# Reordering VectorE's queue around transferred states, and a third group of seven-product up tiles, in a one-core SSM + GLU kernel

## The chip, the cores and the metric

One core of one Trainium2 chip. The metric is the device time in microseconds (us) of one execution. All runs told here were in the fast state, with a granted TensorE clock between 0.998 and 1.0. Besides the time, each run gives the **span**: the time from the first to the last instruction that the profile sees.

## The reference, cut to what matters

```python
xn  = layernorm(x)                      # x: 2048 tokens x 512
Bu  = einsum("bld,pd->blp", xn, B_bar)  # complex, 512 states
h   = Lam_bar * h + Bu[:, t]            # 2048 steps in a row
y   = 2 * einsum("blp,dp->bld", hseq, Cmat).real + xn * Dskip
mlp = (silu(xn @ w1) * (xn @ w3)) @ w2  # 512 -> 1792 -> 512
out = x + y + mlp
```

The first part is a state space model (SSM: 512 complex states, stepped through the tokens), the second a gated linear unit (GLU: a gate tile times an up tile, then w2). The kernel takes the tokens in four blocks of 512, each of four chunks of 128. Per block it makes the gate and up tiles (14 of each, 128 features by 512 tokens), rotates the inputs of the states, scans them, rotates them back ("posts": two multiplications and an add per half of the states), and then makes the outputs for two pairs of chunks (pairs 0 to 7 in all) from gated features and states. Several of the products use a seven-product scheme in place of eight: fewer matmuls, more sums on VectorE. An "eviction" is the sum or copy that takes a finished result out of TensorE's accumulation bank.

## The kernel before: what the change and the argument touch

The order of VectorE's instructions is decided while the program is built. Work that can wait stands in a list with an estimated cost; at marked places `fill` takes from the list as long as VectorE, by these estimates, is no more than `lead` ahead of TensorE. VectorE then runs what it got in that order.

```python
class Filler:                       # cut: __init__, first, pop, flush
    def add(self, cost, fn, key=None):
        self.tasks.append((cost, fn, key))
    def tensor(self, us):            # TensorE's own clock, in estimates
        self.pe += us
    def own(self, us, after=0.1):    # an instruction put in directly
        self.dve = max(self.dve, self.pe + after) + us
    def fill(self, lead=None):
        limit = self.pe + (self.lead if lead is None else lead)
        while self.tasks and self.dve + 0.5 * self.tasks[0][0] <= limit:
            ...
            self.pop()
        self.dve = max(self.dve, self.pe - 1.0)
```

The add that ends a post is a transfer with accumulation, issued by GpSimd (`act<-p` in the profile), except for the last half of block 3:

```python
def post_c(csl=slice(0, CPB)):
    a, p16 = act_state(b, hf)[:, csl], st["p16"][:, csl]
    if (b, hf) == (NBLK - 1, 1):
        nc.vector.tensor_tensor(out=a, in0=a, in1=p16, op=ALU.add)
    else:
        gp.dma_start(out=a, in_=p16, accum_op=ALU.add)
```

The sums of a pair of chunks read those states. Two of the three are on VectorE (in pairs 1, 6 and 7 the third as well; that branch is cut):

```python
three = (0.9, subtract(s3, a11, a21), ("sums", n))
two   = (0.9, subtract(s2, s3, a22), ("sums", n))
one   = (0.0, lambda: gp.dma_start(out=a21, in_=a22, accum_op=ALU.add), ("sums", n))
```

The last block's gate and up stage: plain tiles first, then `NG` groups of four up tiles by seven products each. `s4` and the two adds (evictions that `add` makes) are on VectorE between the products that need them:

```python
for n in range(NG):
    ...
    product(g, a11, b11, True);  copy(f, g)
    product(e, s1n, t1, True);   copy(s5, e)
    gate_side(f0, upper[0])
    bg.fill(1.2)
    gates.pop()()
    product(f, a12, b21, False)
    product(g, s2n, t2, False);  copy(e, g)
    bg.own(0.42)
    nc.vector.tensor_tensor(out=s4n, in0=a12, in1=s2n, op=ALU.subtract)
    ...
    gate_side(f0 + 1, upper[0])
    bg.fill()
    product(g, s3n, t3, False);  copy(z, g)
    add(lower[1][:, :, TH:TBLK], g)
    product(e, s4n, b22, False)
    add(upper[1][:, :, TH:TBLK], e)
    ...
```

Where pair 4's sums are put in the list (`middle` comes between the rotations of block 3's first half and those of its second, two multiplications each; `between` comes after both):

```python
last_posts = ssm_tasks(3, middle=[(0.0, after_y2, None), *row_sums(4, *pairs[4])])
```

## Time and profile before

| | before |
|---|---|
| time, median of the first 3 runs | 202.15 us (202.10 to 202.42) |
| span of the profiled run | 200.7 us |
| TensorE busy | 195.3 us, 97% |
| VectorE busy | 179.6 us, 89%, 256 instructions |
| ScalarE busy | 134.5 us, 67% |
| first gate matmul of block 0 | starts at 12.80 us |
| last matmul | starts at 197.74 us |

What lies before the first gate matmul (loads, layernorm, transposes) came out between 12.2 and 13.1 us in the profiles of this study, whatever the kernel. From that matmul to the start of the last one, which I call the **steady stretch**, the kernel before takes 197.74 - 12.80 = 184.94 us. Three more profiles of the same schedule give 185.03, 184.94 and 185.04. A change of 0.1 us can be read from it, while the times of one kernel's runs in one call lie 0.3 to 1.2 us apart.

The views that carry the prediction are shown in it. One more belongs here, the first line of the chain that ended last, as shares of the span:

```profile
PE 86%; DMA 5%; DVE 5%; issue 1%; SPq 1%; DVEq 0%
```

The 5% of DMA and the 5% of DVE say that the end of the program hangs somewhere on VectorE and on transfers, and not on matmuls alone.

### The profile page before, as it was taken

To read this page: it belongs to the slowest core of one execution; us is meant where nothing else is said; L and a number is where in the kernel's file an instruction comes from. 1 tells how busy PE (TensorE), PEld (TensorE's weight loads), DVE (VectorE), ACT (ScalarE), POOL (GpSimd) and SP (SyncE) were. 2 spreads that over 40 slices of the span, in tenths; PEclk is the share of its full clock that TensorE was granted. 3 is DMA by queue.
4 is the path that set the end of the run, shared out by engine and by line. 5 is a ranking of instruction groups with operands and counts; after the bars stand their busy time and mean duration, and the time that the engine had idled before them with its cause. 6 is when DMAs were issued, how large, how long until landed. Compare 5 with 4: busy or idle time off the path is not lost.

```text
span 200.7 us, 3660 instructions
## 1 busy us (share of the span) xinstructions
PE 195.3 (97%) x1376; PEld 129.4 (64%) x1389; DVE 179.6 (89%) x256; ACT 134.5 (67%) x279; POOL 49.9 (25%) x75
## 2 busy tenths in 40 slices
PE   8899999999999999999999999999999999999994
PEld 2774444444444488855565478888445568888893
DVE  3599699999999999989899998999996989999952
ACT  4699797699999987868997674451668783111220
POOL 7170279800411143031202115030032103310000
PEclk9999999999999999999999999999999999999999
DMA  6999995990398046721997187747159511990111
GB/s 165 321 265 221 303 169 112 339 278 7 57 180 152 0 91 121 131 81 32 171 114 104 30 152 129 172 75 105 52 73 178 111 28 30 187 159 30 52 41 42
DMA packets 32514, 25.38 MB, mean 126 GB/s; under 512 B 16240, under 2 KB 30192, under 8 KB 32496
## 3 DMA queue, kind: packets, MB, share of 16 engines
q0 software_dynamic: 6384, 11.64, 34.2%
q1 hardware_dynamic: 25536, 13.21, 27.4%
q10 hardware_dynamic: 576, 0.30, 0.7%
q8 instruction: 11, 0.18, 0.4%
q14 instruction: 7, 0.06, 0.1%
HBM read 7.74 MB, written 2.10 MB: 49 GB/s over the span
## 4 chain that ended last, share of the span: by engine, by line
PE 86%; DMA 5%; DVE 5%; issue 1%; SPq 1%; DVEq 0%
PE gu_ps L580 33%; PE gu_ps L1039 17%; PE y_ps L1039 10%; PE bu_ps L1039 7%; PE y_ps L450 3%; PE bu_ps L450 3%; PE y_ps L766 3%; DMA act<-p 3%; DMA w_sb<-in_B_w_dram 2%; PE gu_ps L834 2%; PE gu_ps L612 2%; PE gu_ps L766 2%; PE bu_ps L766 1%; PE y_ps L855 1%; PE bu_ps L612 1%
## 5 line engine op out<-in xcount | busy, mean ns | idle before, releaser
L580 PE MATMUL gu_ps<-xnT,w_sb 128*128 128x512 bf16 x304 | 68.9, 379 | 0.4
L580 PEld LDWEIGHTS <-w_sb 128*128 128x128 bf16 x312 | 30.5, 98 | 34.2
L1039 PEld LDWEIGHTS <-act 128*128 128x128 f16 x462 | 43.5, 98 | 5.5
L589 ACT ACTIVATE g<-gu_ps 128x512 bf16<-128x512 f32 x41 | 24.8, 604 | 5.2 <-PE gu_ps L580 3.2
L590 ACT ACTIVATE u<-gu_ps 128x512 bf16<-128x512 f32 x41 | 24.9, 606 | 4.8 <-PE gu_ps L580 4.5
L503 DVE TENSOR_TENSOR_SCAN u<-rho,ends,u 128x512 bf16<-128x512 f32 x16 | 20.2, 1274 | 0.0
L834 PE MATMUL gu_ps<-xnT,w_sb 128*128 128x512 bf16 x77 | 18.4, 379 | 0.2
L525 POOL DMA_DIRECT2D act<-p x7 | 9.2, 1316 | 36.3 <-DVE act L517 25.2
L1039 PE MATMUL gu_ps<-w_sb,act 128*128 128x256 bf16 (+3 forms) x126 | 15.9, 267 | 0.0
L597 DVE TENSOR_TENSOR act<-g,u 128x1024 f16<-128x1024 bf16 x21 | 14.3, 679 | 0.0
L834 PEld LDWEIGHTS <-w_sb 128*128 128x128 bf16 x80 | 7.8, 98 | 7.5
L846 ACT ACTIVATE g<-gu_ps 128x512 bf16<-128x512 f32 x14 | 8.4, 598 | 6.1 <-PE gu_ps L834 6.0
L450 PEld LDWEIGHTS <-bt 128*128 128x128 bf16 x64 | 6.3, 98 | 7.5
L1039 PE MATMUL bu_ps<-w_sb,act 128*128 128x256 bf16 (+3 forms) x84 | 10.4, 264 | 0.0
L1062 ACT ACTIVATE x_blk<-gu_ps 128x256 f32<-128x256 f32 (+1 forms) x9 | 3.3, 366 | 10.6 <-PE gu_ps L1039 10.6
L1039 PE MATMUL gu_ps<-ct,act 128*128 128x256 f16 (+1 forms) x72 | 10.4, 267 | 0.0
L993 POOL DMA_DIRECT2D act<-act x5 | 4.6, 926 | 21.8 <-DVE tw L986 10.3
L503 DVE TENSOR_TENSOR_SCAN u<-rho,u 128x512 bf16<-128x512 f32 x8 | 9.2, 1207 | 0.0
L1039 PEld LDWEIGHTS <-x_blk 128*128 128x128 f16 x88 | 8.6, 98 | 1.0
L1039 PEld LDWEIGHTS <-tw 128*128 128x128 f16 x88 | 8.6, 98 | 1.0
L486 DVE TENSOR_TENSOR u<-u,tabe 128x2048 bf16<-128x2048 bf16 x7 | 8.6, 1223 | 0.2
L511 DVE TENSOR_TENSOR p<-u,tabe 128x2048 f16<-128x2048 bf16 x7 | 8.5, 1221 | 0.1
(203 smaller groups left out, 384.4 us busy)
## 6 DMA issues: line engine op xcount, KB each, us to landing
act<-p POOLq DMA_DIRECT2D x7, 512.0 KB, 5.8
xn<-x_blk POOLq DMA_DIRECT2D x4, 512.0 KB, 5.5
out_dram<-xn SPq DMA_DIRECT2D x15, 128.0 KB, 1.7
w_sb<-in_B_w_dram SPq DMA_DIRECT2D x1, 1792.0 KB, 8.6
act<-act POOLq DMA_DIRECT2D x5, 352.0 KB, 4.3
w_sb<-in_B_w_dram SPq DMA_DIRECT2D x2, 768.0 KB, 6.1
u<-p POOLq DMA_DIRECT2D x3, 512.0 KB, 5.6
w_sb<-in_B_w_dram SPq DMA_DIRECT2D x4, 256.0 KB, 4.7
```

Source lines behind the costliest of these rows:

```text
L450: nc.tensor.matmul(out=ps, lhsT=bt[:, ri, dt, pt * P:(pt + 1) * P], rhs=xnT_blk[b][:, dt, :], start=(dt == 0), stop=(dt == NDT - 1))
L486: nc.vector.tensor_tensor(out=st["g"], in0=st["g"], in1=tabe[:, psl, 0:1, :].to_broadcast(FULL), op=ALU.mult)
L503: nc.vector.tensor_tensor_scan(out=v, data0=rho[:, pt:pt + 1].to_broadcast([P, TBLK]), data1=v, initial=init, op0=ALU.mult, op1=ALU.add)
L511: nc.vector.tensor_tensor(out=by_state(st["p16"][:, csl]), in0=by_chunk(st["g"][:, :, ::-1, tsl]), in1=by_chunk(tabe[:, psl, 2:0:-1, tsl]) ...
L525: gp.dma_start(out=a, in_=p16, accum_op=ALU.add)
L580: nc.tensor.matmul(out=ps[:, tsl], lhsT=w[:, dt, f * P:(f + 1) * P], rhs=xnT[:, dt, tsl], start=(dt == 0), stop=(dt == NDT - 1))
L589: nc.scalar.activation(out=g16[:, f % 2, :], in_=g_ps, func=ACT.Silu)
L590: nc.scalar.activation(out=u16[:, f % 2, :], in_=u_ps, func=ACT.Copy)
L597: nc.vector.tensor_tensor(out=act_gates(b, f - 1), in0=split(g16), in1=split(u16), op=ALU.mult)
L766: nc.tensor.matmul(out=out[:, h * TH:(h + 1) * TH], lhsT=left[:, h, k, :], rhs=right[:, k, :], start=(start and h == 0 and k == 0), stop=( ...
L834: nc.tensor.matmul(out=ps, lhsT=w[:, dt, f * P:(f + 1) * P], rhs=xnT[:, dt, :], start=(dt == 0), stop=(dt == NDT - 1))
L1039: nc.tensor.matmul(out=out, lhsT=left[:, k, :], rhs=right[k][:, cols], start=(start and k == 0), stop=(k == NK - 1), skip_group_check=True)
```

## The change

The intent: take a wait for a transfer out of VectorE's in-order queue by putting pair 4's sums (and in block 2, pair 2's) behind work that needs no transfer; spread block 3's posts so that pair 6 waits for half of them only; and use the seven-product scheme on 12 up tiles instead of 8. Some estimates of the list are lowered, too.

```diff
-    NG = 2
+    NG = 3
-    LEAD = 2.0
+    LEAD = 1.7
 ...  (post_c)
-                if (b, hf) == (NBLK - 1, 1):
+                if b == NBLK - 1 and (hf == 1 or csl.start > 0):
                     nc.vector.tensor_tensor(out=a, in0=a, in1=p16, op=ALU.add)
 ...  (block 3's posts)
-        add(*post0, *scans1)
-        early, late = ([... for fn in post1] for h in range(2))
-        for t in early:
+        def by_tokens(fns, h):
+            part = slice(h * CPB // 2, (h + 1) * CPB // 2)
+            return [(0.0 if fn is post0[2] and h == 0 else 0.6, lambda fn=fn: fn(part), ("ssm", b)) for fn in fns]
+        for t in by_tokens(post0, 0):
             bg.add(*t)
-        return late
+        add(*scans1)
+        for t in by_tokens(post1, 0):
+            bg.add(*t)
+        return by_tokens(post0, 1) + by_tokens(post1, 1)
 ...  (up groups)
-            bg.fill(1.2)
+            bg.fill(0.8)
 ...  (order of the lists)
-    ssm_tasks(2, between=[(0.2, lambda: keep_ends(1)), *row_sums(2, *pairs[2])], late=res_list(3) + column_sums(3))
+    ssm_tasks(2, between=res_list(3), late=[(0.2, lambda: keep_ends(1)), *row_sums(2, *pairs[2]), *column_sums(3)])
-    last_posts = ssm_tasks(3, middle=[(0.0, after_y2, None), *row_sums(4, *pairs[4])])
+    last_posts = ssm_tasks(3, between=[(0.0, after_y2, None), *row_sums(4, *pairs[4])])
```

Cut: the estimated costs of four kinds of work (posts, column sums, pair sums, input sums), lowered by 0.04 to 0.2; a branch that is never taken; and a table `ORDER` whose entries are the order that was already used.

More of the change, by code (lines that the diff above doesn't have):

```diff
@@ L475, in pre_a @@
                     st["p"] = up.tile(FULL, BF16, name="u")
-                elif b > 3:
-                    st["p"] = x_blk[b].rearrange("p (j r) t -> p j r t", r=2)
                 elif b == NBLK - 1:
@@ L538, in add @@
             for fn in fns:
-                bg.add(0.0 if fn in transfers else 1.2, fn,
+                bg.add(0.0 if fn in transfers else 1.2 if fn in scans0 or fn in scans1 else 1.16, fn,
                        ("scan", b) if fn in scans0 else ("post", b) if fn in post0 else ("ssm", b))
@@ L565, in ssm_tasks @@
             return
-        add(*post0, *scans1)
-        early, late = ([(0.6, lambda fn=fn, h=h: fn(slice(h * CPB // 2, (h + 1) * CPB // 2)), ("ssm", b)) for fn in post1]
-                       for h in range(2))
-        for t in early:
+        def by_tokens(fns, h):
+            part = slice(h * CPB // 2, (h + 1) * CPB // 2)
+            return [(0.0 if fn is post0[2] and h == 0 else 0.6, lambda fn=fn: fn(part), ("ssm", b)) for fn in fns]
+        for t in by_tokens(post0, 0):
             bg.add(*t)
-        return late
+        add(*scans1)
+        for t in by_tokens(post1, 0):
+            bg.add(*t)
+        return by_tokens(post0, 1) + by_tokens(post1, 1)
     def glu(b):
@@ L705, in column_sums @@
         run.ready = lambda: ("norm", b, CPB - 1) in sins_done
-        return [(1.7, run, "cols")]
+        return [(1.5, run, "cols")]
     def column_list(b):
@@ L743, in bu_sums @@
         first = [t for two in zip(tasks[0], cols) for t in two]
-        return [(0.42, lambda out=out, x=x, y=y, op=op: nc.vector.tensor_tensor(out=out, in0=x, in1=y, op=op), ("bu", hf))
+        return [(0.36, lambda out=out, x=x, y=y, op=op: nc.vector.tensor_tensor(out=out, in0=x, in1=y, op=op), ("bu", hf))
                 for hf, part in ((0, first), (1, tasks[1])) for out, x, y, op in part]
@@ L986, in subtract @@
             return lambda: nc.vector.tensor_tensor(out=out, in0=x, in1=z, op=ALU.subtract)
-        three = (0.9, subtract(s3, a11, a21), ("sums", n))
-        two = (0.9, subtract(s2, s3, a22), ("sums", n))
+        three = (0.84, subtract(s3, a11, a21), ("sums", n))
+        two = (0.84, subtract(s2, s3, a22), ("sums", n))
         if n in (1, 6, 7):
-            one = (0.9, lambda: nc.vector.tensor_tensor(out=a21, in0=a21, in1=a22, op=ALU.add), ("sums", n))
+            one = (0.84, lambda: nc.vector.tensor_tensor(out=a21, in0=a21, in1=a22, op=ALU.add), ("sums", n))
         else:
@@ L1019 @@
     later = {}
+    ORDER = {4: (1,4,2,6,5,7,3), 5: (1,4,2,6,5,7,3), 6: (1,4,2,6,5,7,3)}
     def y_fast(n, then=(), between=()):
@@ L1131, in y_fast @@
         products = (product1, product2, product3, product4, product5, product6, product7)
-        for i in ((1, 5, 2, 6, 4, 3, 7) if b == 0 else (1, 2, 4, 6, 5, 7, 3) if b == 1 else (1, 4, 2, 6, 5, 7, 3)):
+        for i in ((1, 5, 2, 6, 4, 3, 7) if b == 0 else (1, 2, 4, 6, 5, 7, 3) if b == 1 else ORDER.get(n, (1, 4, 2, 6, 5, 7, 3))):
             if i == 3 and n in LATER:
```

## The prediction

> **What bounds the kernel now.** I read the page first, the engines' busy shares and the 40 slices.
>
> ```profile
> PE 195.3 (97%) x1376; PEld 129.4 (64%) x1389; DVE 179.6 (89%) x256; ACT 134.5 (67%) x279; POOL 49.9 (25%) x75
> PE   8899999999999999999999999999999999999994
> DVE  3599699999999999989899998999996989999952
> ```
>
> TensorE is busy in every slice from the second to the last but one, and VectorE is close behind. Since a busy TensorE may still be waiting inside its modelled ends, I looked next at who waited for whom, for TensorE alone:
>
> ```profile
> PE bu_ps L196 <- PEq L1253: 0.8, 1, 0.8
> PE gu_ps L612 <- DMA w_sb<-in_B_w_dram: 0.6, 1, 0.6
> PE y_ps L855 <- DVE u L865: 0.2, 1, 0.2
> PE y_ps L243 <- DVE xn L224: 0.2, 1, 0.2
> PE y_ps L855 <- DVE w_sb L896: 0.2, 1, 0.2
> ```
>
> The first, second and fourth lie in the first 13 us, which the change does not touch. Two waits are left, both in the last block's gate and up stage (lines 834 and 855). The time line of TensorE there shows their true size in the distance between starts:
>
> ```profile
> 153.66 0.60 PE L855 MATMUL y_ps<-x_blk,w_sb 128*128 128x256 f16 x4
> 154.43 0.61 PE L855 MATMUL y_ps<-xnT,w_sb 128*128 128x256 bf16 x4 [0.17 <-DVE w_sb L896]
> ...
> 156.18 1.03 PE L834 MATMUL gu_ps<-xnT,w_sb 128*128 128x512 bf16 x4
> 157.43 0.60 PE L855 MATMUL y_ps<-xnT,w_sb 128*128 128x256 bf16 x4 [0.22 <-DVE u L865]
> 158.02 0.60 PE L855 MATMUL y_ps<-x_blk,bt 128*128 128x256 f16 x4
> 158.46 1.03 PE L834 MATMUL gu_ps<-xnT,w_sb 128*128 128x512 bf16 x4
> ```
>
> Undisturbed, four 256-column matmuls take 0.44 us from start to start (158.02 to 158.46), four 512-column ones 0.86. So 153.66 to 154.43 holds 0.33 us of stall, 156.18 to 157.43 holds 0.39, and 157.43 to 158.02 0.15: 0.87 in all. Elsewhere between 13 us and the last matmul at 197.7 I found no start-to-start distance longer than the shape needs, except single distances of twice a 512-column matmul, which are missing records. Why VectorE was late is in its own time line:
>
> ```profile
> 149.80 0.88 DVE L986 TENSOR_TENSOR x_blk<-act 128x1408 f16<-128x1408 f16 x1
> 152.54 0.89 DVE L986 TENSOR_TENSOR x_blk<-x_blk,act 128x1408 f16<-128x1408 f16 x1 [1.86 <-DMA act<-p]
> 153.35 0.69 DVE L850 TENSOR_TENSOR act<-g,u 128x1024 f16<-128x1024 bf16 x1
> 153.95 0.42 DVE L896 TENSOR_TENSOR w_sb<-w_sb,bt 128x512 f16<-128x512 bf16 x1
> ```
>
> VectorE runs in order. A sum of pair 4 that nobody needs before 162 us waited 1.86 us for a state transfer, and the sum s4 (L896) that TensorE needed at 154.1 stood behind it. The two evictions at 156.69 (L865) were late from the same backlog. This is the target of the change.
>
> **What the Trainium skill says.** "TensorE: Matmul & The Clock Gate", Back-to-back issue gap, gives N/2.4 + 2.5 ns a matmul warm: 216 ns at 512 columns, 109 at 256. The trace agrees (0.86/4 and 0.44/4 us). "Perfetto Trace Analysis", Identifying the Most-Contended Engine, warns that matmul busy time does not show distance from roofline; weight loads are busy only 64% here. I therefore use the distance of starts, by which the array is full. "VectorE: DVE Perf Modes", The perf-mode tier table, has a 16-bit tensor_tensor at 2048 elements at 1224 ns; the trace has 1221 (L511). "DMA: Bandwidth & Descriptors", SWDGE vs HWDGE vs iDMA, says that an accumulating transfer must be issued from GpSimd; here act<-p needs 5.8 us from issue to landing (median), which is what has to be kept off VectorE's queue.
>
> **The change, part by part.**
>
> Up scheme on 12 tiles. The seven-product scheme replaces four plain up tiles more: 16 matmuls of 512 columns (4 x 0.86 = 3.46 us) by 7 x 4 matmuls of 256 (7 x 0.437 = 3.06). TensorE saves 0.40 us, the only matmul work that goes; all other matmuls keep number and order. It costs ScalarE two more copies (six for four, 0.6 each; it is 67% busy). It costs VectorE one more s4 (0.42), two more evictions (1.2 together), and three input sums of 1536 instead of 1024 columns: 0.69 at 1024, 0.885 at 1408 and 1.09 at 1792 give about 0.95, so 3 x 0.27 = 0.8. Together 2.4 us of VectorE.
>
> Pair 4's sums behind the two rotations and the first gates. In the new order L896 of the first group no longer follows L986. Followed with the old durations (independent neighbours start 0.08 us before the former's end): TensorE enters the stage at 139.8 as before and reaches the first group after four plain tiles at 143.26. VectorE starts the input sums at 140.34, ends them at about 143.1, then the two posts, difference and gate, and s4 is done near 146.7. TensorE wants it at 147.2: 0.4 us to spare. First evictions at about 147.8 to 149.1, wanted at 149.8 and 150.2. For groups two and three s4 is ready near 152.9 and 158.4, wanted at 153.7 and 160.2. Pair 4's first sum now comes near 155, the transfer lands near 152. So all 0.87 us of stall should go, and L986 should wait for nothing.
>
> The same in block 2 (pair 2's sums and the keep of the states behind the skip product, L919). Old: 0.65 us of VectorE idle for act<-p before L1200; new: filled by L919. TensorE did not wait there, so nothing is gained directly. The smaller costs and the shorter LEAD only reorder neighbours; following the queue from 91 us, I find VectorE back in step with the old time line at the add near 132.4 (old 132.51), since it must wait there for TensorE's products anyway.
>
> Half of block 3's posts behind pair 6's sums. Pair 6 needs the first two chunks only, so two 1.22 us posts become four of 0.68 (+0.12 us at start-to-start distance), the first half's transfer shrinks from 512 KB, and the second half's add moves from a transfer to VectorE (0.69). The test is whether VectorE's extra work still fits. From TensorE's start of pair 4 (162.8 instead of 164.1): VectorE idles about 1 us before the add of product 2, which now comes ahead of pair 5's sum, then ends the second state half of pair 6 at 178.8 (wanted 180.3, as the state rows are the 8th weight tile), pair 6's sums at 181.2 (wanted 182.0; old margin only 0.4), and in pair 7 the last state half at 189.2 (wanted 189.9), second sum at 190.9 (wanted 191.6), third at 191.7 (wanted 192.8). Tight, yet no stall. Old VectorE sat idle 1.58 us before pair 7's L1081, and that room is what is spent.
>
> Sum: 202.15 - 0.40 - 0.87 = 200.88. Start and final store stay. I add 0.07 for small waits where margins are under 0.5 us: 200.95.
>
> **Rivals.** (1) The stall merely moves: with three groups, each with its s4 and evictions, VectorE comes late again, as 2.4 us of work are added to an engine at 89%. For: the first group now begins 6.9 us earlier (143.26 instead of 150.16), just behind the input sums, with 0.4 us to spare. Against: the 1.86 us wait goes, nearly as much as is added. It would return 0.3 to 0.9 us: 201.2 to 201.8. (2) VectorE becomes the bound in pairs 6 and 7, where my margins are 0.7 to 1.1 us and the walk has an error of about as much. One lost microsecond of VectorE before that would show as up to 0.5 us: about 201.4. (3) The removed DMA wait was hidden anyway and only the matmuls count: 201.75. Against it, TensorE's 0.33 us names L896 directly, and only 0.42 + 0.69 us of VectorE lay between it and the DMA wait. (4) A large gain, because VectorE's idle shrinks everywhere: ruled out, as TensorE is full from start to start; no more than 1.3 us can go without removing matmuls.
>
> **Range and chances.** The floor is 200.88 less run noise (the three runs span 0.32): 200.6. Above, rivals 1 and 2 together reach about 201.7. Two per cent are 4.04 us; nothing on the list is that large on either side. Faster 0.01, within 0.98, slower 0.01.
>
> **What would show it.** Right: line 855's group has 84 matmuls instead of 56, line 834's plain ones 16 fewer; no TensorE wait of over 0.1 us on L896 or L865 (old numbers); L986 with no DMA wait; the last matmul about 1.3 us earlier, near 196.5; VectorE busy up by about 3 us to near 183. Wrong: a new TensorE wait for VectorE in the first group (s4), or in pair 6 or 7 (state rows, second sum), or a wait of evicted banks anywhere from 87 to 140 us, where the order of VectorE changed too.

## The result, and the profile after

| | before | after |
|---|---|---|
| time, median of 4 runs each | 202.24 us (202.10 to 202.42) | 201.54 us (201.25 to 201.66) |
| span of the profiled run | 200.7 | 199.3 |
| steady stretch | 184.94 | 183.68 |
| time minus span | about 1.8 | 2.15 to 2.26 |
| VectorE busy | 179.6, x256 | 182.6, x262 |

The ratio is 0.9963, 95% interval 0.9946 to 0.9980. Ratios here are the mean time of one kernel's fast runs over that of the other's of the same rounds, so not quite the ratio of the medians that I quote. The change is faster by 0.7 us where I had predicted 1.2; the stretch that I had walked through is shorter by 1.27 (the rounded figures give 1.26), which is what I had predicted.

The lines after that answer to those before. Most line numbers are three or four higher: L858, L868, L899 and L989 are the old L855, L865, L896 and L986. Those of the posts are two lower: L509, L515 and L521 are the old L511, L517 and L523. First the busy shares and VectorE's slices from the page of the changed kernel, and the first line of its chain:

```profile
PE 195.4 (98%) x1401; PEld 130.6 (66%) x1401; DVE 182.6 (92%) x262; ACT 134.9 (68%) x281; POOL 51.3 (26%) x75
DVE  3699799999999999989999997999999999999972
...
PE 95%; DMA 2%; SPq 1%; issue 0%; DVE 0%
```

Most of VectorE's dips in the second half are filled (a 7 is left), and VectorE (5% before) has left the chain. TensorE's waits in the whole changed kernel are two, both in the start phase:

```profile
PE bu_ps L196 <- PEq L1257: 0.8, 1, 0.8
PE gu_ps L615 <- DMA w_sb<-in_B_w_dram: 0.4, 1, 0.4
```

TensorE's time line in the first of the three up groups (start, duration, then the instructions). The product with s4 is the one at 147.09; the next group, which needs the evicted banks, begins at 149.69:

```profile
146.65 0.60 PE L858 MATMUL y_ps<-x_blk,w_sb 128*128 128x256 f16 x4
147.09 0.60 PE L858 MATMUL y_ps<-xnT,w_sb 128*128 128x256 bf16 x4
147.52 1.03 PE L837 MATMUL gu_ps<-xnT,w_sb 128*128 128x512 bf16 x4
...
148.82 1.03 PE L837 MATMUL gu_ps<-xnT,w_sb 128*128 128x512 bf16 x4
149.69 0.60 PE L858 MATMUL y_ps<-xnT,w_sb 128*128 128x256 bf16 x4
```

The distance of starts is 0.44 and 0.43 around the product with s4, and 0.87 from 148.82 to 149.69: nothing but the shapes, and no bracket. And VectorE over the same stage and in the last two pairs:

```profile
146.18 0.42 DVE L899 TENSOR_TENSOR w_sb<-w_sb,bt 128x512 f16<-128x512 bf16 x1
...
148.12 1.29 DVE L868 TENSOR_TENSOR u<-y_ps,bt 128x512 bf16<-128x512 f32 x2 [0.38 <-ACT bu_ps L846]
...
155.86 0.88 DVE L989 TENSOR_TENSOR x_blk<-act 128x1408 f16<-128x1408 f16 x1
...
157.26 0.89 DVE L989 TENSOR_TENSOR x_blk<-x_blk,act 128x1408 f16<-128x1408 f16 x1
...
178.16 0.68 DVE L521 TENSOR_TENSOR act<-act,p 128x1024 f16<-128x1024 f16 x1
...
188.52 0.68 DVE L521 TENSOR_TENSOR act<-act,p 128x1024 f16<-128x1024 f16 x1
```

Pair 4's sum (L989) has no bracket any more: it waits for no transfer. In the walk I had s4 done at 146.7 (here 146.60), the evictions from 147.8 to 149.1 (148.12 to 149.41), L989 near 155 (155.86), pair 6's state half done at 178.8 (178.84), pair 7's at 189.2 (189.20). The matmul count answers too: weight loads of plain tiles, the group of line 834 before and of 837 after, fall by 16.

```profile
L834 PEld LDWEIGHTS <-w_sb 128*128 128x128 bf16 x80 | 7.8, 98 | 7.5
```

```profile
L837 PEld LDWEIGHTS <-w_sb 128*128 128x128 bf16 x64 | 6.2, 98 | 4.8
```

The evictions came 0.3 us later than in the walk because they waited for a copy on ScalarE (`<-ACT bu_ps L846`), which the walk had left out; the bank was still in time. So the steady stretch went as predicted to the tenth, and yet the time did not fall by as much. The difference is in the row "time minus span". That was the first question for the experiments; the second was which part of the change did what.

### The profile page after: what moved, and what is told of

It is laid out like the page before. It is cut to its first block, busy times and chain, and to the rows that moved or that the text cites. A ratio compares the mean times of both kernels' runs of the same rounds, so it can differ in the third digit from the quotient of the medians.

```text
span 199.3 us, 3709 instructions
## 1 busy us (share of the span) xinstructions
PE 195.4 (98%) x1401; PEld 130.6 (66%) x1401; DVE 182.6 (92%) x262; ACT 134.9 (68%) x281; POOL 51.3 (26%) x75
## 4 chain that ended last, share of the span: by engine, by line
PE 95%; DMA 2%; SPq 1%; issue 0%; DVE 0%
PE gu_ps L583 34%; PE gu_ps L1043 17%; PE y_ps L1043 10%; PE gu_ps L837 7%; PE bu_ps L1043 7%; PE y_ps L450 3%; PE bu_ps L450 3%; PE y_ps L858 3%; PE y_ps L769 3%; DMA w_sb<-in_B_w_dram 2%; PE gu_ps L615 2%; PE gu_ps L769 2%; PE bu_ps L858 1%; PE bu_ps L769 1%; PE bu_ps L615 1%; SPq L166 0%
## 5 line engine op out<-in xcount | busy, mean ns | idle before, releaser
L583 PE MATMUL gu_ps<-xnT,w_sb 128*128 128x512 bf16 x312 | 69.6, 379 | 0.0
L583 PEld LDWEIGHTS <-w_sb 128*128 128x128 bf16 x312 | 30.5, 98 | 34.2
L523 POOL DMA_DIRECT2D act<-p x7 | 9.2, 1321 | 33.9 <-DVE act L515 21.9
L837 PE MATMUL gu_ps<-xnT,w_sb 128*128 128x512 bf16 x64 | 15.9, 379 | 0.0
L837 PEld LDWEIGHTS <-w_sb 128*128 128x128 bf16 x64 | 6.2, 98 | 4.8
L509 DVE TENSOR_TENSOR p<-u,tabe 128x2048 f16<-128x2048 bf16 (+1 forms) x8 | 8.7, 1085 | 0.0
L515 DVE TENSOR_TENSOR act<-u,tabe 128x2048 f16<-128x2048 bf16 (+1 forms) x8 | 8.7, 1085 | 0.0
```

The source lines that it names most:

```text
L509: nc.vector.tensor_tensor(out=by_state(st["p16"][:, csl]), in0=by_chunk(st["g"][:, :, ::-1, tsl]), in1=by_chunk(tabe[:, psl, 2:0:-1, tsl]) ...
L515: nc.vector.tensor_tensor(out=by_state(act_state(b, hf)[:, csl]), in0=by_chunk(st["g"][:, :, :, tsl]), in1=by_chunk(tabe[:, psl, 0:1, tsl] ...
L583: nc.tensor.matmul(out=ps[:, tsl], lhsT=w[:, dt, f * P:(f + 1) * P], rhs=xnT[:, dt, tsl], start=(dt == 0), stop=(dt == NDT - 1))
L837: nc.tensor.matmul(out=ps, lhsT=w[:, dt, f * P:(f + 1) * P], rhs=xnT[:, dt, :], start=(dt == 0), stop=(dt == NDT - 1))
```

## The experiments

Twelve kernels, in three calls. Each call used one chip and shared eleven runs of the kernel before: medians 202.33, 202.28 and 202.24. All kernels were correct. Theories A (the stall of 0.87 us is in every run of the kernel before, and its end is worth that much) and B (it is peculiar to the profiled run) are the first pair.

### First call: is the stall there, and which part ends it?

**The kernel before once more.** No edit.

> The kernel before, unchanged, once more: what one trace of it is worth. Theory A (the 0.87 us of TensorE stall in the up stage is there in every run): its spans lie near 200.7 us, the difference of time and span is the same as the changed kernel's (about 2.2 us), its second trace has the same two waits (0.33 on L896, 0.39 + 0.15 on L865), and it takes 202.2 us. Rival B (the stall hangs on when the state transfer lands and is smaller in most runs, so the profiled run was an unlucky one): the spans of the timed runs lie near 200.0, the new trace has a stall clearly under 0.87. Rival C: the time outside the span differs between the kernels.

Measured: 202.22 us (202.12 to 203.34), ratio 0.9999 (0.9975 to 1.0022). The stall is there again, 0.32 + 0.38 + 0.17 = 0.87 us, with the same two named instructions, and VectorE's wait of 1.9 for `act<-p`. Two more profiles of this schedule in the third call show it as well (0.87 and 0.96). B falls.

**Only pair 4's sums moved.**

```diff
-    last_posts = ssm_tasks(3, middle=[(0.0, after_y2, None), *row_sums(4, *pairs[4])])
+    last_posts = ssm_tasks(3, between=[(0.0, after_y2, None), *row_sums(4, *pairs[4])])
```

> The kernel before with only block 3's queue changed: pair 4's sums behind the two rotations of the second half. Theory A: L896 no longer behind L986, TensorE has no wait on L896 or L865 of 0.1 us or more, time 0.87 us less, 201.35. Rival B: the stall also goes in the trace, but the time falls by only 0.3 to 0.5. Rival D (with two groups the sums or the evictions are late for another reason): a new wait for VectorE takes the place, time as before.

Measured: 201.46 us (201.07 to 201.52), ratio 0.9949 (0.9930 to 0.9967), so about 0.9 to 1.0 us less. The steady stretch is 184.12 us against 184.94 to 185.04, so 0.82 to 0.92 less. One changed word gives the whole 0.87. VectorE's time line of this run shows how:

```profile
152.58 0.42 DVE L896 TENSOR_TENSOR w_sb<-w_sb,bt 128x512 f16<-128x512 bf16 x1
152.92 0.88 DVE L986 TENSOR_TENSOR x_blk<-act 128x1408 f16<-128x1408 f16 x1
...
156.13 0.88 DVE L986 TENSOR_TENSOR x_blk<-x_blk,act 128x1408 f16<-128x1408 f16 x1
```

s4 (L896) stands ahead of both sums, and is done at 153.0, where it had begun at 153.95 before.

**Only the third group, nothing moved.**

```diff
-    NG = 2
+    NG = 3
```

> The kernel before with only the up scheme on 12 instead of 8 tiles. Matmul work falls by 0.40 us. Theory A as I wrote it (pair 4's sums stall the queue where they stand): the stall stays or grows to about 1 us, time 201.8 to 202.3. Rival E (the third group alone reorders the queue, since it changes what the filler lets in: in the program's order L986 now comes after the second group's L896 and the transfer has landed): stall gone too, 1.2 us less in the trace, time about 201.0 to 201.5.

Measured: 203.10 us (202.94 to 203.90), ratio 1.0043 (1.0018 to 1.0068): alone, the part that saves matmuls makes the kernel slower by 0.8 us (steady stretch 185.72). The stall of the up stage has gone, as rival E said: the group lets pair 4's sums in only behind the second s4 (L896, done at 153.24), at 153.16 and 154.07, and the second of them no longer waits for the transfer:

```profile
154.07 0.89 DVE L986 TENSOR_TENSOR x_blk<-x_blk,act 128x1408 f16<-128x1408 f16 x1
```

But neither theory foresaw the price: VectorE's work for the group (2.4 us in the prediction; its busy time is 182.4 us against 179.6) comes back at pair 6. The lines are its TensorE wait, TensorE at that place, and VectorE there:

```profile
PE gu_ps L1039 <- DVE act L523: 1.6, 1, 1.6
```

```profile
179.60 0.93 PE L1039 MATMUL gu_ps<-tw,act 128*128 128x256 f16 x7
182.16 0.61 PE L1039 MATMUL gu_ps<-tw,act 128*128 128x256 f16 x4 [1.64 <-DVE act L523]
```

```profile
178.32 1.27 DVE L503 TENSOR_TENSOR_SCAN x_blk<-rho,act,x_blk 128x512 bf16<-128x512 f32 x1
...
181.41 0.69 DVE L523 TENSOR_TENSOR act<-act,p 128x1024 f16<-128x1024 f16 x1
```

The last scan of block 3 begins at 178.32 here, 1.3 us later than in the kernel before (176.98), and the state half that pair 6's product needs at about 180.3 is ready at 182.1.

**The changed kernel with two groups.**

```diff
-    NG = 3
+    NG = 2
```

> The changed kernel with the up scheme back on 8 tiles. Theory A: 0.40 us of matmul more than the changed kernel, no stall: 0.4 us slower than it, about 201.9 by its measured 201.54. If the third group costs TensorE something that I do not see, the two would be equal.

Measured: 201.60 us (201.16 to 202.12), ratio 0.9962 (0.9941 to 0.9983), no slower than the whole change, where I had expected 0.4 us more. Its profile holds a stall of 0.61 us that I had not expected, at the start of block 2:

```profile
85.06 1.36 PE L1043 MATMUL gu_ps<-tw 128*128 128x256 f16 x11
86.86 1.90 PE L583 MATMUL gu_ps<-xnT,w_sb 128*128 128x512 bf16 x7 [0.44 <-DMA xnT<-xn]
```

TensorE waits for a transposing transfer there. No other profile shows it, so it belongs to that run or to that version; this stays open. The steady stretch is 184.68 us; less the stall it would be 184.07, against 184.12 of the move alone. So the rest of the change without the third group (block 2's new order, the lower costs and `LEAD`, the split posts), which was not tried part by part on the kernel before, makes no more than 0.05 us of difference together. The time outside the span was 1.82 us on average, not 2.2. That was the second hint that the time outside depends on the program and not on the day.

### Second call: the changed kernel's parts, and the time outside the span

C1 says that the extra time outside the span belongs to the changed program, C2 that it came with the chip or the session of that first measurement.

**The changed kernel once more.** No edit.

> The changed kernel, unchanged, beside the kernel before on one chip. So far its time was 2.2 us over its span, the kernel before's 1.8 (on this and on the other chip), so that 0.4 us of its gain vanish outside the span. Theory C1 (that belongs to the program): span 199.3, time 201.5 again. Rival C2 (it belongs to the chip or the session of that first run): span 199.3, time 201.1, gain 1.2 us.

Measured: 201.83 us (201.44 to 201.91), ratio 0.9970 (0.9956 to 0.9983); time minus span 2.11 to 2.23 in all five runs, while the eleven runs of the kernel before on the same chip had 1.74 to 1.94. C2 falls. The steady stretch is 183.68 again; the start phase of this profile took 13.09 us.

**The changed kernel with pair 4's sums in their old place.**

```diff
-    last_posts = ssm_tasks(3, between=[(0.0, after_y2, None), *row_sums(4, *pairs[4])])
+    last_posts = ssm_tasks(3, middle=[(0.0, after_y2, None), *row_sums(4, *pairs[4])])
```

> The changed kernel with pair 4's sums back ahead of the rotations of the second half. In its program order L989 then stands before the second group's s4 and evictions. Theory A: L989 waits 0.5 to 0.9 us for act<-p again, and s4 and the evictions of the second group come 0.3 to 0.7 us late in all: time 0.3 to 0.7 over the changed kernel's of the same rounds. Rival: the shorter LEAD alone keeps the queue fit, no stall, time as the changed kernel's.

Measured: 201.34 us (201.04 to 201.80), ratio 0.9952 (0.9937 to 0.9968), no stall at all, and a steady stretch of 183.68. My expectation was wrong. (That its median is 0.49 us below the changed kernel's is no gain of the schedule: stretch and time outside the span are the same, and the start phase took 12.39 us in this profile, 13.09 in that one.) The same instruction's line in the kernel before, and two lines of this run:

```profile
144.73 1.22 DVE L517 TENSOR_TENSOR act<-u,tabe 128x2048 f16<-128x2048 bf16 x1
```

```profile
143.80 1.22 DVE L515 TENSOR_TENSOR act<-u,tabe 128x2048 f16<-128x2048 bf16 x1
...
150.75 0.88 DVE L989 TENSOR_TENSOR x_blk<-act 128x1408 f16<-128x1408 f16 x1
```

Block 2's last post starts 0.93 us earlier, so its transfer does as well (issued at 145.57 against 146.50). The first of the two sums comes 1 us later than in the kernel before (150.75 against 149.80), and the second, the one that had waited 1.86 us and began at 152.54, begins at 152.49 without a wait, as a gate and an s4 now stand between the two. The first group's s4 was done at 146.3, ahead of both. In the kernel before, the move alone is enough; in the changed kernel it is not needed. My rival named `LEAD` as the reason, and that is not shown: the third group alone, with the old lead, had no such stall either.

**The changed kernel with block 3's first-half posts whole.**

```diff
-                if b == NBLK - 1 and (hf == 1 or csl.start > 0):
+                if (b, hf) == (NBLK - 1, 1):
 ...
-        for t in by_tokens(post0, 0): ...
+        add(*post0, *scans1)      # as in the kernel before; only post1 in two halves
```

> The changed kernel with block 3's posts of the first half whole again, ahead of pair 6. The kernel before with 12 tiles alone lost 1.8 us at pair 6's state rows. Theory F (the third group's 2.4 us of VectorE are paid by the split posts): the second half's states (L521) end about 180.6, TensorE wants them at 180.3, and pair 6's second sum near 182.9 against 182.3: a stall of 0.7 to 1.0 us in pair 6, time 0.7 to 1.0 over the changed kernel's. Rival: the lower costs and LEAD are what avoids that loss, the split does nothing: time as the changed kernel's.

Measured: 201.68 us (201.39 to 201.96), ratio 0.9964 (0.9950 to 0.9978). The profile has the stall where I looked for it, but smaller: 0.38 + 0.08 us at pair 6; the steady stretch is 184.16, 0.48 over the changed kernel's. The wait and its cause:

```profile
PE gu_ps L1039 <- DVE act L521: 0.2, 1, 0.2
```

```profile
179.82 0.69 DVE L521 TENSOR_TENSOR act<-act,p 128x1024 f16<-128x1024 f16 x1
```

The half is done at 180.51 instead of 178.84. So the split is worth about half a microsecond of the stretch. The time doesn't show it: this program had only 1.96 to 2.02 us outside its span, 0.17 less than the changed kernel on average, and the rest is within the scatter of the start phase.

**The changed kernel with the old lead.**

```diff
-    LEAD = 1.7
+    LEAD = 2.0
```

> The changed kernel with LEAD at 2.0 as before. In its program order the first group's evictions (L868) stand behind both rotations of the first half instead of one: by the trace they would end at 149.6 and 150.2, TensorE wants the banks at 149.7 and 150.1. Theory: a stall of 0.1 to 0.3 us at the second group's start, time 0.1 to 0.3 over the changed kernel's. Rival: LEAD is of no matter, equal.

Measured: 203.36 us (203.21 to 203.54), ratio 1.0050 (1.0037 to 1.0063). The place that I had named has 0.12 us of stall, but a far larger one, 1.87 us, lies in pair 3. Its wait, and GpSimd's issues in this run and in the changed kernel:

```profile
PE bu_ps L1043 <- DMA act<-tw: 1.7, 1, 1.7
```

```profile
133.07 1.29 POOL L523 DMA_DIRECT2D act<-p  x1 [9.87 <-PE gu_ps L769]
133.83 1.45 POOL L1082 DMA_DIRECT2D act<-tw  x1
```

```profile
131.98 0.86 POOL L1082 DMA_DIRECT2D act<-tw  x1 [8.85 <-PE bu_ps L1043]
132.75 1.41 POOL L523 DMA_DIRECT2D act<-p  x1
```

VectorE's order at this place is the same in both. With the old lead the large state transfer (512 KB) is issued ahead of the sum that pair 3 is waiting for. That sum (352 KB) is issued 1.85 us later and then needs 6.6 us to land instead of 3.8. The lead matters here, by the order of transfers in GpSimd's queue; I had looked on VectorE alone. It isn't the lead by itself, though: the kernel before has the same lead of 2.0 and issues the sum first (at 132.07, the state transfer at 134.35). The bad order needs the old lead together with something else of the change, such as the lower costs; which, was not tried.

### Third call: what makes the time outside the span?

The traces begin and end alike. What differs is the number of records that each engine has in the trace, with those that are not counted as busy. TensorE's and ScalarE's counts are the same in the kernel before with three groups (1.79 us outside) as in the changed kernel (2.16), so they are not it. VectorE's were 305 to 308 in the programs with 1.8, 310 in the one with 1.99, and 311 or 312 in those with 2.14 to 2.20. Theory C-vec: VectorE's count is the cause. C-other: something else of the changed kernel.

**The kernel before with six tiny memsets on VectorE**, where it is idle at the start.

```diff
+    pad = const.tile([P, 8], FP32, name="pad")
+    for i in range(6):
+        nc.vector.memset(pad[:, i:i + 1], 0.0)
```

> The kernel before with six tiny extra memsets on VectorE at its very start, where VectorE is idle; no other line differs. The question is the time outside the profiled span (time minus span), which was 1.74 to 1.87 us in every kernel with up to 307 VectorE records in the trace (before 305, the two-group one 307), about 2.0 with 310 and 2.1 to 2.2 with 312. Theory C-vec (it grows with the number of VectorE's instructions in the program): here about 311 records, so 2.05 to 2.2 us outside the span, span as before (200.4), time 202.5 to 202.7, ratio about 1.0015. Rival C-other (something else of the changed kernel, not its count): stays 1.75 to 1.87 and the time 202.2.

Measured: 202.52 us (202.14 to 202.83), ratio 1.0015 (0.9999 to 1.0031); outside the span 2.11 to 2.23 in every run, mean 2.15, against 1.80 (1.74 to 1.90) for the kernel before on the same chip. The time alone doesn't tell this from noise, the time outside the span does. The span is unchanged (mean 200.40 and 200.44), the steady stretch 184.94. The memsets themselves are over at 0.99 us, long before VectorE's first real instruction at 3.04:

```profile
0.79 0.20 DVE L200 MEMSET pad<- 128x1 f32 x6 [0.79 <-PEq L1257]
```

**Six tiny activations on ScalarE instead.**

```diff
+    pad = const.tile([P, 8], FP32, name="pad")
+    for i in range(6):
+        nc.scalar.activation(out=pad[:, i:i + 1], in_=ones[:, i:i + 1], func=ACT.Copy)
```

> The kernel before with six tiny extra activations on ScalarE near its start: the control for the run with six on VectorE. C-vec: 1.75 to 1.87 us outside the span, time 202.2 to 202.4. A theory in which any engine's count, or the program's total, matters: 2.0 us or more outside the span, time 202.5 or more.

Measured: 202.23 us (201.85 to 202.54), ratio 0.9997 (0.9982 to 1.0012); outside the span 1.73 to 1.86. So it is not the program's total, and not simply the count of whatever engine. Whether ScalarE has such a step at another count was not tried.

**The changed kernel with six VectorE instructions fewer.** The angles of two tables are made together; only the first step, with its own scalar per table, stays apart.

```diff
-        nc.vector.tensor_scalar(out=rnd, in0=ang, scalar1=MAGIC, scalar2=None, op0=ALU.add)      # one table
+        two = [scratch[:, i * 2 * TBLK:(i + 2) * 2 * TBLK].bitcast(FP32) for i in (pt, NPT + pt)]
+        nc.vector.tensor_scalar(out=two[1], in0=two[0], scalar1=MAGIC, scalar2=None, op0=ALU.add)  # two tables
 ...  (the two steps after it likewise; table_angles(0) and (2) make (1) and (3) too)
```

> The changed kernel with the angles of two tables made by one instruction instead of two (three instructions for each pair of tables, six fewer VectorE instructions in all, about 306 records). C-vec: 1.75 to 1.87 us outside the span and, with a span of 199.3, a time of 201.1 to 201.2, ratio about 0.9945, lower than the changed kernel's 201.54. C-other: 2.1 to 2.2 outside and 201.5. Risk: the second pair's sines may come some tenths of a us later in the start, which the span would show.

Measured: 201.12 us (200.81 to 201.62), ratio 0.9948 (0.9932 to 0.9965); outside the span 1.75 to 1.88, mean 1.80. The steady stretch is the changed kernel's, 183.68. The busy line of its page (compare x262 above):

```profile
PE 195.7 (98%) x1401; PEld 131.3 (66%) x1401; DVE 181.9 (91%) x256; ACT 134.8 (68%) x281; POOL 51.8 (26%) x75
```

**The same, with pair 4's sums in their old place** (both edits shown above).

> As the run before, with pair 4's sums in their old place as well (the run of the changed kernel without the move had a span of 198.9 to 199.7 and 2.10 to 2.23 us outside it, 201.34). C-vec: 1.75 to 1.87 outside the span, time 200.9 to 201.1, ratio about 0.994. C-other: 2.1 to 2.2, time 201.35.

Measured: 200.98 us (200.89 to 201.34), ratio 0.9941 (0.9927 to 0.9955); outside 1.74 to 1.88, mean 1.79. Steady stretch 183.68. This and the one before are faster than the kernel before in the same rounds, though still "same" at 2%; the two can't be told apart, as their intervals overlap. The changed kernel was not run in this call. Its ratios were 0.9963 and 0.9970, and their intervals overlap with that of the six fewer alone (0.9932 to 0.9965), so that the two beat it as well is likely by the time outside the span, but not shown by the times.

C-vec holds in all four, in both directions. Mean time outside the span by VectorE's records:

| VectorE records | programs | mean outside, us |
|---|---|---|
| 305 | before, its repeat, move only, six on ScalarE | 1.77 to 1.82 |
| 306 | six fewer; six fewer without the move | 1.80, 1.79 |
| 307 | changed with two groups | 1.82 |
| 308 | before with three groups | 1.79 |
| 310 | changed with whole posts | 1.99 |
| 311 | before with six memsets; old lead | 2.15, 2.14 |
| 312 | changed, its repeat, changed without the move | 2.16 to 2.20 |

It is not a price per instruction: 305 to 308 cost the same, and the rise comes between 308 and 311. Whether it goes on rising above 312 was not tried. The Trainium skill, "Runtime: NRT & Kernel Launch", Instruction fetch mechanics, says that an engine's program is fetched in blocks of 256 instructions and that crossing a block boundary is "mostly hidden". A boundary that VectorE's program crosses would give such a step. No run here shows this: the page counts the same 11 and 7 instruction transfers within the span before and after. And 308 to 311 records in a trace are no multiple of 256; how many instructions of the program leave no record isn't known. It stays an argument.

## Why the prediction was right or wrong, point by point

- **TensorE bound, stall of 0.87 us removable: right, shown.** The repeat has the same stall, the move alone ends it (184.94 to 184.12 us), and the changed kernel has none.
- **0.40 us of matmuls from the third group: right, shown.** The move alone, with two groups and no stall, has a steady stretch of 184.12; the changed kernel, with three, 183.68. That is 0.44.
- **Their sum, 1.27 us: right for the stretch that it was worked out for.** 184.94 - 183.68 = 1.26, or 1.27 before rounding.
- **The walk along VectorE's queue: right within 0.1 us for the first s4 and in pairs 6 and 7**, where the margins were 0.4 to 1.5 us. It was 0.3 early for the first evictions (they waited for ScalarE) and the second group's s4 (done at 153.21), 0.7 for the third's (159.08), and 0.9 for L989. No margin was used up.
- **Pair 4's move as the reason that the stall goes: half right.** It is enough in the kernel before. In the changed kernel the stall would be gone without it, as the run without the move shows. The third group is a cure as well: alone, with the sums in their old place, it ended the stall, though it paid at pair 6. Two cures were in the change, and the prediction credited one.
- **The split of the posts: right.** Without it pair 6 stalls by 0.46 us.
- **Rivals.** None of the three came true in the changed kernel. Rival 2, VectorE as the bound in pair 6, comes as soon as a part is missing: the third group alone stalls 1.8 us there, the change without the split 0.46.
- **"The smaller costs and the shorter LEAD only reorder neighbours": right for the change as a whole, and not safe for its parts.** VectorE was back in step at the add at 132.37 (predicted 132.4). But the lead reaches further than VectorE: with the old one, in the changed kernel, GpSimd issues two transfers in the other order, which costs 1.99 us of the steady stretch (185.67 against 183.68). The prediction did not look at the order of transfers; that the version walked through had the right one is luck.
- **"Start and final store stay", with the time taken as 202.15 less what the stretch loses: the step that failed.** The start and the store stayed within the scatter; that nothing else would change was the mistake. The time outside the span went from 1.80 to about 2.17 us. It is not in the trace, and no walk along queues could have found it. Put in: 202.24 - 1.27 + 0.37 = 201.34; measured 201.54 in the first four runs and 201.83 in the next five, of which the rest, 0.2 to 0.5, is as large as the scatter of single runs and of the start phase, and I leave it there (in the call of the five, the mean span fell by 0.98 us, from 200.56 to 199.58, with a late start in the profiled run). That 201.54 lies in the stated range is luck in part: the room above 200.95 was left for rivals 1 and 2, which didn't come, and it was filled by a cost that was not on the list. With the count of VectorE's instructions put back, the changed schedule takes 200.98 to 201.12, where the prediction had 200.95.

One citation left out its limit: the section "Back-to-back issue gap" gives N/2.4 + 2.5 ns for the isolated gap and another figure for a stream of matmuls. The formula is the one that the trace supports (last section).

What the change costs in all: it adds six busy VectorE instructions, three by the third group and three by the split posts. The third group's 0.44 us of matmuls is hence nearly paid back outside the span (2.20 with it, 1.82 without, in different calls), which fits that the version with two groups measured no slower in spite of the stall in its profile.

## What to carry to other kernels

When the instruction that holds up an in-order engine is a sum over transferred data that nobody needs yet, move that sum; one changed line gave 0.87 us here, and more matmul savings without room on VectorE gave minus 0.8. Compare a stretch that starts behind the noisy start phase, by the distance of starts, but check the time minus the span as well: a gain of 1.27 us in the trace was 0.7 in the time, and six VectorE instructions fewer took the time outside the span back from about 2.17 to 1.80 us. Where a scheduler with estimates decides the order, look at the order of transfers on the issuing engine too, not only at the order on the engine that computes.

## What the Trainium skill lacked or had wrong

- "TensorE: Matmul & The Clock Gate", Back-to-back issue gap, states about 131 ns a matmul at 512 columns for a stream of weight loads and matmuls. The stream here (1389 weight loads to 1376 recorded matmuls) took 0.86 us from start to start for four such matmuls, about 216 ns each.
- "Runtime: NRT & Kernel Launch" tells of fixed costs around a kernel and of a fetch that is mostly hidden. It lacks that the number of one engine's instructions can show in the time while the trace stays the same: six memsets on an idle VectorE took the time outside the span from 1.80 to 2.15 us (305 to 311 records), six activations on ScalarE left it at 1.77.
- "DMA: Bandwidth & Descriptors", Anatomy of one DMA — SWDGE (gpsimd) path, fits 2.0 us plus bytes over 436 GB/s, which gives an estimate of 3.2 us for 512 KB. The accumulating transfers `act<-p` of that size took 5.8 us from issue to landing (median of seven), so the fit doesn't serve for them here. Whether the accumulation or the other transfers under way make the difference was not tried.
- I found no figure on any page for what a transfer loses when a larger one is issued just ahead of it on GpSimd: `act<-tw`, 352 KB, landed after 3.8 us when it was first and after 6.6 us behind 512 KB, counted from its own issue.
